# Input casts and transposes moved to the DMA in a kernel of attention and a long convolution

## The chip, the cores and the metric

The kernel runs on one core of one Trainium2 chip. The time is that of the device for one execution, in microseconds. Inputs and output lie in the chip's memory (DRAM); the weights and q, k, v are float32, the matrix products take bfloat16 operands.

## What is computed

```python
# attention: B=4, H=8, S=768, D=64; heads 0, 2 and 6 causal, the others
# causal with only the first 4 keys and a window of 64 kept
scores = (q @ k.T) / 8
a = softmax(where(mask[head], scores, -1e9))
x = (a @ v)                  # [4, 8, 768, 64] -> [4, 768, 512]
# second part: D=512
proj = x @ w_proj            # [512, 1536]
x1, x2, x3 = split(proj, 3)
conv = irfft(rfft(x2, axis=seq) * rfft(filter, axis=seq))
out = (x1 * conv * x3) @ w_out
```

## The kernel before

**Attention.** Two heads of one batch make a pair; there are 16 pairs, four for each batch, and the main loop runs over them. For each pair `emit_loads` (L99) brings q, k and v as float32 on the queue of SyncE (SP), with a sequence position on each partition: 128 partitions, six tiles of 128 positions. `emit_cast` (L269) turns q and k into bfloat16 with the two heads side by side, on VectorE. `emit_prep` (L284) makes `qkT`, in which the 2 x 64 head dimensions lie on the partitions and the 768 positions along the row: six 128x128 TensorE transposes into a PSUM bank for q and six for k, each followed by a VectorE copy into SBUF. `emit_v` (L275) casts v on POOL into `v_aug`, which has a column of ones, and multiplies by a head mask into `v_far`.

`emit_chunk` (L293) computes scores for four 128x128 blocks of both heads at a time (six chunks in a pair), takes the exponential on ScalarE into `pT`, and multiplies the masked blocks on VectorE. `emit_values` (L323) multiplies with v, in which the column of ones gives the sum, and divides on VectorE into `attn`. `emit_turn` (L341) transposes `attn` with six TensorE transposes and a VectorE copy into a quarter of `xT`, the transposed attention output of a batch.

**Second part.** `moe` (L349) is a generator that is advanced one step after each chunk, so that its work for batch b-1 lies among the attention of batch b. It folds the sequence in two (`xf`, two VectorE additions), projects x2 (L358), transforms it with the real matrix `G` (`emit_forward`, L212), multiplies by the transformed filter `HAB`, computes x1 and x3 and their product (L390, L399), transforms back with `Gi` (L406), multiplies, projects (L419) and stores on SP (L423). A batch has 22 steps, about the length of four and a half pairs. After the last pair the second part of the last batch runs alone.

**Setup.** `G` holds sines and cosines that ScalarE computes from iotas made by POOL. `Gi` is made from `G` by 18 TensorE transposes and three VectorE copies (L226). The transformed filter `HAB` comes from `setup_steps` (L225), a generator that starts with the third pair.

**Order.** Within each engine and each queue instructions start in the order that a scheduler derives from the order of the program and the dependences; VectorE and POOL have the written order in the setup. An instruction that waits holds up all that is queued behind it on its engine or queue. The buffers of loaded inputs are three, of `qkT`, `v_aug` and `attn` two. The loads of pair n+2 are issued in pair n (L462). The weights and the filter, which a DMA casts to bfloat16, are issued on POOL's queue in the second pair; `hold` (L95) writes one element of the destination first, so that such a DMA waits until a given pair's `v_aug` is there. The fifth pair's q load is held in the same way.

```python
if c == (1 if n else 3) and nxt:      # L468: casts of the next pair
if c == 2 and last:                   # L473: emit_turn of the pair before
if c == (3 if n else 4) and nxt:      # L477: qkT of the next pair
```

Of the kernel before, what the change touches and what calls it, by code (L numbers as in the profile page):

```python
# [9 lines left out]
FP32 = mybir.dt.float32  # L10
BF16 = mybir.dt.bfloat16
# [32 lines left out]
def kernel(  # L44
# [13 lines left out]
    nc = tc.nc  # L58
# [33 lines left out]
    ret_i64 = const.tile([128, H], mybir.dt.int64, name="ret_i64")  # L92
    nc.sync.dma_start(out=ret_i64, in_=is_retrieval.partition_broadcast(128))

    def hold(first, n):  # L95

        nc.gpsimd.tensor_copy(out=first, in_=state[n]["v_aug"][:, 0, 0, 0:1])

    def emit_loads(b, hp, behind=None):  # L99
        qk = ald.tile([128, 2, 2, NT, D], FP32, name="qk_f32")  # L100
        vf = ald.tile([128, 2, NT, D], FP32, name="v_f32")
        if behind is not None:
            hold(qk[:, 0, 0, 0, 0:1], behind)
        for dst, src in ((qk[:, 0], q), (qk[:, 1], k), (vf, v)):
            nc.sync.dma_start(
                out=dst, in_=src[b, 2 * hp:2 * hp + 2].rearrange("h (t p) d -> p h t d", p=128))
        return qk, vf

    PREFETCH = 2
# [93 lines left out]
    def emit_matrix():  # L203

        nc.gpsimd.tensor_scalar(out=G[:, :, 1, 0], in0=par.to_broadcast([128, NM]), scalar1=-2.0, scalar2=1.0,
                                op0=ALU.mult, op1=ALU.add)
        nc.gpsimd.tensor_copy(out=G[:, :, 6:8, 0:64], in_=G[:, :, 4:6, 64:128])
        nc.gpsimd.tensor_copy(out=G[:, :, 6:8, 64:128], in_=G[:, :, 4:6, 0:64])

    Gi = const.tile([128, 6, HS], BF16, name="Gi")  # L210

    def emit_forward(src, tiles):  # L212

# [9 lines left out]
    HA, HB = HAB[:, :, 0:2, :], HAB[:, :, 2:4, :]  # L223

    def setup_steps():  # L225
        for t in range(0, 6, 2):  # L226
            ps = bank("gi_ps", [128, 2, HS], BF16)
            for u in range(2):
                for m in range(NM):
                    nc.tensor.transpose(ps[:, u, m * 128:(m + 1) * 128], G[:, m, t + u, :], identity)  # L230
            nc.vector.tensor_copy(out=Gi[:, t:t + 2, :], in_=ps)
            yield
        yield
        yield
        fold = msb.tile([128, 2, NM, DM], BF16, name="fold", tag="x2")
        with tc.issue_after(state[3]["first"].ins):
            nc.vector.tensor_add(fold[:, 0], filt[:, 0:NM, :], filt[:, NM:NT, :])
            nc.vector.tensor_sub(fold[:, 1], filt[:, 0:NM, :], filt[:, NM:NT, :])

        def put(engine, out, in_, w):  # L240
            if engine is nc.scalar:
                engine.activation(out=out, in_=in_, func=AF.Copy, scale=w / S)
            else:
                engine.tensor_scalar(out=out, in0=in_, scalar1=w / S, scalar2=None, op0=ALU.mult)

        for t in range(2):
            ps = emit_forward(fold, ((2 * t, t), (2 * t + 1, t)))
            put(nc.scalar, HAB[:, t, 0:4:3, :], ps, 2.0)
            nc.gpsimd.tensor_scalar(out=HB[:, t, 0, :], in0=HB[:, t, 1, :], scalar1=-1.0, scalar2=None,
                                    op0=ALU.mult)  # L250
            nc.gpsimd.tensor_copy(out=HA[:, t, 1, :], in_=HA[:, t, 0, :])
            if t == 0:
                nc.gpsimd.tensor_scalar(out=HA[0:1, 0, 1, :], in0=HB[0:1, 0, 1, :], scalar1=0.5, scalar2=None,
                                        op0=ALU.mult)
                nc.gpsimd.tensor_scalar(out=HA[0:1, 0, 0, :], in0=HA[0:1, 0, 0, :], scalar1=0.5, scalar2=None,
                                        op0=ALU.mult)
                nc.gpsimd.memset(HB[0:1, 0, :, :], 0.0)
            yield
        plain = emit_forward(fold, ((4, 0), (5, 1)))
        put(nc.scalar, HA[0:64, 2, :, :], plain[0:64, :, :], 2.0)  # L260
        put(nc.vector, HB[64:128, 2, :, :], plain[64:128, :, :], 2.0)
        yield
        swapped = emit_forward(fold, ((6, 0), (7, 1)))
        put(nc.scalar, HA[64:128, 2, :, :], swapped[64:128, :, :], 2.0)
        put(nc.vector, HB[0:64, 2, :, :], swapped[0:64, :, :], -2.0)
        yield


    def emit_cast(engine, st, a):  # L269
        if a == 0:  # L270
            st["bf"] = asb.tile([128, 2, NT, 2, D], BF16, name="qk_bf")
        qk = loads[st["pair"]][0]
        engine.tensor_copy(out=st["bf"][:, a], in_=qk[:, a].rearrange("p hh t d -> p t hh d"))  # L273

    def emit_v(st):  # L275
        vf = loads.pop(st["pair"])[1]
        st["v_aug"] = v_aug = asb.tile([128, NT, 2, 65], BF16, name="v_aug")
        nc.gpsimd.memset(v_aug[:, :, :, 64:65], 1.0)  # L278
        nc.gpsimd.tensor_copy(out=v_aug[:, :, :, 0:64], in_=vf.rearrange("p hh t d -> p t hh d"))
        st["v_far"] = v_far = asb.tile([128, 4, 2, 65], BF16, name="v_far")  # L280
        hp = st["pair"][1]
        nc.gpsimd.tensor_mul(v_far, v_aug[:, 0:4], vmask[:, hp, :, :, None].to_broadcast([128, 4, 2, 65]))  # L282

    def emit_prep(st):  # L284
        st["qkT"] = qkT = asb.tile([128, 2, S], BF16, name="qkT")
        for a in range(2):
            ps = bank("qkT_ps", [128, S], BF16)
            for t in range(NT):
                nc.tensor.transpose(ps[:, t * 128:(t + 1) * 128],  # L289
                                    st["bf"][:, a, t].rearrange("p hh d -> p (hh d)"), identity)  # L290
            nc.vector.tensor_copy(out=qkT[:, a], in_=ps)  # L291

    def emit_chunk(st, c):  # L293
        qkT = st["qkT"]
# [44 lines left out]
                             rec[:, :, None].to_broadcast([128, NT, 64]))  # L339

    def emit_turn(st):  # L341
        ps = bank("xt_ps", [128, S], BF16)
        for i in range(NT):
            nc.tensor.transpose(ps[:, i * 128:(i + 1) * 128],
                                st["attn"][:, i].rearrange("p hh d -> p (hh d)"), identity)
        nc.vector.tensor_copy(out=st["xT"][:, st["pair"][1], :], in_=ps)


    def moe(b, xT):  # L349
# [51 lines left out]
        for cb in range(NC):  # L401
            ch = slice(cb * 128, (cb + 1) * 128)
            ps = bank_pair("c_ps")
            for r in range(2):
                for n, (tile_no, t, u) in enumerate(((2 * r, r, 0), (2 * r + 1, r, 1), (4 + r, 2, r))):
                    nc.tensor.matmul(ps[:, r, 0:HS], lhsT=P[:, t, u, ch], rhs=Gi[:, tile_no, :],  # L406
                                     start=(n == 0), stop=(n == 2))
            evs = msb2.tile([128, HS], FP32, name="evs")
            nc.scalar.copy(out=evs, in_=ps[:, 0, 0:HS])
            conv = msb2.tile([128, S], BF16, name="conv")  # L410
            nc.vector.tensor_add(conv[:, 0:HS], evs, ps[:, 1, 0:HS])  # L411
            nc.vector.tensor_sub(conv[:, HS:S], evs, ps[:, 1, 0:HS])
            nc.vector.tensor_mul(y[:, cb, :], conv, g[:, cb, :])  # L413
            yield
# [10 lines left out]
            yield  # L425


    emit_cast(nc.vector, state[0], 0)
    emit_mask(0)
    emit_mask(1)  # L430
    emit_cast(nc.vector, state[0], 1)
    emit_prep(state[0])
    emit_v(state[0])
    setup_order.__exit__(None, None, None)
    loads[pairs[1]] = emit_loads(*pairs[1])
# [12 lines left out]
    for n, (b, hp) in enumerate(pairs):  # L448
# [11 lines left out]
        for c in range(len(CHUNKS)):  # L460
            emit_chunk(st, c)
            if c == (0 if n < 2 else 3) and n + 2 < len(pairs):  # L462
                loads[pairs[n + 2]] = emit_loads(*pairs[n + 2], behind=3 if n == 2 else None)
            if c == 0 and last:
                emit_values(last, 0)
            if c == 1 and last:
                emit_values(last, 1)
            if c == (1 if n else 3) and nxt:  # L468
                with tc.issue_after(st["first"].ins):
                    for a in range(2):  # L470
                        emit_cast(nc.vector, nxt, a)
                emit_v(nxt)
            if c == 2 and last:  # L473
                emit_turn(last)
                if hp == 0:
                    gates.append(moe(b - 1, last["xT"]))
            if c == (3 if n else 4) and nxt:  # L477
                emit_prep(nxt)
            if c == 4 and n == 1:
                filt = msb.tile([128, NT, DM], BF16, name="filt", tag="xf")  # L480
                hold(filt[:, 0, 0:1], 2)
                nc.gpsimd.dma_start(out=filt, in_=moe_filter_fft.rearrange("(t p) c -> p t c", p=128))
                w = moe_w_proj.rearrange("(c p) n -> p c n", p=128)
                for part in (1, 0, 2):
                    cols = slice(part * DM, part * DM + DM)
                    hold(wproj[:, 0, part * DM:part * DM + 1], 2)
                    nc.gpsimd.dma_start(out=wproj[:, :, cols], in_=w[:, :, cols])
                hold(wout[:, 0, 0:1], 2)
                nc.gpsimd.dma_start(out=wout, in_=moe_w_out.rearrange("(c p) n -> p c n", p=128))
            if c < 5:  # L490
                gate_step()
# [44 lines left out]
```

## Time and profile before

| what | value |
|---|---|
| runs | 260.65, 262.06, 263.44 us; median 262.06 |
| profiled execution | 261.73 us, span 260.0 us |
| granted TensorE clock | 0.958 |
| L289 transposes of q and k, PE | 192, 16.6 us busy |
| L344 transposes of attn, PE | 96, 8.1 us |
| L273 casts of q and k, VectorE | 32, 20.9 us |
| L291 copies into qkT, VectorE | 32, 16.8 us |
| L346 copies into xT, VectorE | 16, 8.8 us |
| L279 casts of v, POOL | 16, 15.1 us |
| q, k and v loads on SP | 48 of 384 KB, median 5.1 to 6.0 us from issue to landing |
| DMA | 28.36 MB, 80,822 packets, 74,912 of them under 512 bytes |

The span reaches from the first to the last instruction. PE is TensorE's matmul side, PEld its weight loads, DVE is VectorE, ACT ScalarE, POOL GpSimd, SP SyncE; a q after an engine's name means its sequencer or queue. A line such as L289 is a line of the kernel. A share of DMA is the mean share of 16 DMA engines; the sum of the packets' times can exceed 1 where the packets of several queues overlap. The chain of work that ended last is followed back from the last instruction to whatever released each step.

### The profile page before, as it was taken

The page shows a single profiled execution, that of the slowest core. Times are in us where ns is not written, and L with a number is a line of the kernel's source. Part 1 is how long each engine was busy: PE and PEld are TensorE (multiplying, and loading weights), DVE is VectorE, ACT ScalarE, POOL GpSimd, SP SyncE. Part 2 cuts the span into 40 slices and gives each one's busy share as a digit, 9 for nine tenths or more (in the row PEclk, how much of TensorE's full clock was granted, in tenths as well). Part 3 has the DMA queues.
Part 4 walks back from the last instruction along what each step waited for, and adds up shares of the span by engine and source line. Part 5 has one row for each costly group of instructions (what it writes and reads, how often), then busy time and mean ns, then how long its engine had stood idle before and what let it go on. Part 6 is the DMA issues. An engine that isn't in the chain of part 4 may idle for free.

```text
span 260.0 us, 4624 instructions
## 1 busy us (share of the span) xinstructions
PE 217.1 (83%) x1898; PEld 111.9 (43%) x1898; DVE 178.9 (69%) x349; ACT 153.7 (59%) x182; POOL 52.3 (20%) x83
## 2 busy tenths in 40 slices
PE   0286957386999899989998999899999998999980
PEld 0134532144344455544445555344445553446530
DVE  4988785079269958994599669983697596065640
ACT  6577443534488565758686567576885622663431
POOL 4536732913021202020204022011110000000000
PEclk9999797859799999999999999999999999999996
DMA  7999999999608095439636390042000000600005
GB/s 139 218 218 211 178 193 197 203 228 186 118 6 179 0 183 107 78 92 320 144 56 132 52 183 3 0 164 81 0 3 0 5 0 0 245 0 0 0 21 223
DMA packets 80822, 28.36 MB, mean 109 GB/s; under 512 B 74912, under 2 KB 77728, under 8 KB 80800
## 3 DMA queue, kind: packets, MB, share of 16 engines
q1 hardware_dynamic: 77904, 25.18, 46.2%
q0 software_dynamic: 2896, 2.88, 6.7%
q8 instruction: 15, 0.25, 0.4%
q14 instruction: 7, 0.06, 0.1%
HBM read 24.65 MB, written 6.29 MB: 119 GB/s over the span
## 4 chain that ended last, share of the span: by engine, by line
PE 45%; DVE 35%; DMA 9%; ACT 7%; issue 2%; ACTq 0%; DVEq 0%
PE x_ps L390 12%; PE x_ps L358 8%; DMA qk_f<-in_q_dram 7%; PE out_ps L419 5%; PE att L330 5%; PE sc L304 5%; DVE pT L317 4%; DVE qk_bf L273 4%; PE X_ps L217 4%; ACT pT L310 3%; DVE y L413 3%; DVE conv L411 3%; PE qkT_ps L289 3%; DVE attn L338 3%; DVE m L379 2%
## 5 line engine op out<-in xcount | busy, mean ns | idle before, releaser
L310 ACT ACTIVATE pT<-sc 128x1024 bf16<-128x1024 f32 x96 | 86.1, 922 | 24.1 <-PE sc L304 23.7
L390 PE MATMUL x_ps<-xT,wproj 128*128 128x384 bf16 x256 | 46.7, 326 | 0.0
L304 PE MATMUL sc<-qkT 64*128 64x512 bf16 (+3 forms) x256 | 36.3, 332 | 2.7 <-DVE qkT L291 1.4
L317 DVE TENSOR_TENSOR pT<-pT,mask 128x1024 bf16<-128x1024 bf16 x32 | 23.7, 741 | 17.4 <-ACT pT L310 17.1
L330 PE MATMUL att<-v_aug,pT 128*128 128x65 bf16 x352 | 31.6, 198 | 2.2 <-DVE pT L317 1.4
L289 PE MATMUL qkT_ps<-identity,qk_bf 128*128 128x128 bf16 x192 | 16.6, 238 | 19.0 <-DVE qk_bf L273 15.6
L330 PEld LDWEIGHTS <-pT 128*128 128x128 bf16 x672 | 25.0, 99 | 15.5 <-issue 4.8
L390 PEld LDWEIGHTS <-wproj 128*128 128x128 bf16 x256 | 23.3, 98 | 14.3 <-issue 1.3
L278 POOL MEMSET v_aug<- 128x12 bf16 x16 | 3.4, 220 | 122.5 <-PE att L330 122.5
L273 DVE CAST qk_bf<-qk_f 128x768 bf16<-128x768 f32 x32 | 20.9, 665 | 9.1 <-DMA qk_f<-in_q_dram 9.1
L419 PE MATMUL out_ps<-wout,y 128*128 128x512 bf16 x96 | 24.0, 380 | 3.7 <-DVE y L413 2.7
L217 PE MATMUL X_ps<-x,G 128*128 128x512 bf16 x96 | 23.6, 379 | 0.5 <-ACT x L361 0.2
L358 PE MATMUL x_ps<-wproj,xf 128*128 128x512 bf16 x96 | 23.7, 393 | 0.3 <-DVE xf L351 0.3
L304 PEld LDWEIGHTS <-qkT 64*128 64x128 bf16 x256 | 10.9, 96 | 30.2 <-issue 25.9
L330 PE MATMUL att<-v_far,pT 128*128 128x65 bf16 x320 | 23.2, 196 | 0.0
L289 PEld LDWEIGHTS <-qk_bf 128*128 128x128 bf16 x192 | 12.7, 105 | 23.3 <-DVE qk_bf L273 16.6
L397 ACT CAST x1s<-x_ps 128x768 bf16<-128x768 f32 x16 | 12.8, 800 | 15.1 <-PE x_ps L390 13.6
L422 ACT COPY o_sb<-out_ps 128x1024 f32<-128x1024 f32 x12 | 12.1, 1012 | 15.4 <-PE out_ps L419 12.5
L399 DVE TENSOR_TENSOR g<-x1s,x_ps 128x768 bf16<-128x768 bf16 x16 | 15.2, 951 | 8.6 <-PE x_ps L390 6.9
L361 ACT CAST x<-x_ps 128x1024 bf16<-128x1024 f32 x12 | 12.2, 1014 | 13.5 <-PE x_ps L358 13.5
L282 POOL TENSOR_TENSOR v_far<-v_aug,vmask 128x520 bf16<-128x520 bf16 x16 | 18.5, 1153 | 1.2
L338 DVE TENSOR_TENSOR attn<-att,rec 128x384 bf16<-128x384 f32 x32 | 17.7, 552 | 0.4
(80 smaller groups left out, 271.6 us busy)
## 6 DMA issues: line engine op xcount, KB each, us to landing
qk_f<-in_q_dram SPq DMA_DIRECT2D x16, 384.0 KB, 5.1
qk_f<-in_k_dram SPq DMA_DIRECT2D x16, 384.0 KB, 6.0
v_f<-in_v_dram SPq DMA_DIRECT2D x16, 384.0 KB, 5.9
out_dram<-o_sb SPq DMA_DIRECT2D x12, 512.0 KB, 2.9
wproj<-in_moe_w_proj_dram POOLq DMA_DIRECT2D x3, 512.0 KB, 15.7
filt<-in_moe_filter_fft_dram POOLq DMA_DIRECT2D x1, 768.0 KB, 9.9
wout<-in_moe_w_out_dram POOLq DMA_DIRECT2D x1, 512.0 KB, 21.0
ret_i<-in_is_retrieval_dram SPq DMA_DIRECT2D x1, 8.0 KB, 3.1
```

What stands on the lines that cost most here:

```text
L217: nc.tensor.matmul(ps[:, u, :], lhsT=G[:, m, t, :], rhs=src[:, r, m, :], start=(m == 0), stop=(m == NM - 1))
L273: engine.tensor_copy(out=st["bf"][:, a], in_=qk[:, a].rearrange("p hh t d -> p t hh d"))
L282: nc.gpsimd.tensor_mul(v_far, v_aug[:, 0:4], vmask[:, hp, :, :, None].to_broadcast([128, 4, 2, 65]))
L289: nc.tensor.transpose(ps[:, t * 128:(t + 1) * 128], st["bf"][:, a, t].rearrange("p hh d -> p (hh d)"), identity)
L304: nc.tensor.matmul(sc[:, hh, n * 128:(n + cnt) * 128], lhsT=qkT[rows, 1, j * 128:(j + 1) * 128], rhs=qkT[rows, 0, i * 128:(i + cnt) * 128] ...
L310: nc.scalar.activation(out=pT[:, :, 512 * c:512 * c + w], in_=sc[:, :, 0:w], func=AF.Exp, scale=SCALE)
L317: nc.vector.tensor_mul(near[:, :, c - 1:c + 1, 0:256], near[:, :, c - 1:c + 1, 0:256], mask[:, h0:h0 + 2, 1, None, :].to_broadcast([128, 2 ...
L330: nc.tensor.matmul(att[:, i, :], lhsT=st["pT"][:, hh, at:at + 128], rhs=st["v_far" if i >= j + 2 else "v_aug"][:, j, hh, :], start=(j == 0 ...
L338: nc.vector.tensor_mul(st["attn"][:, :, hh, :], att[:, :, 0:64], rec[:, :, None].to_broadcast([128, NT, 64]))
L358: nc.tensor.matmul(ps[:, r, :], lhsT=xf[:, cc, r, m * 128:(m + 1) * 128], rhs=wproj[:, cc, DM:2 * DM], start=(cc == 0), stop=(cc == NC - 1))
L390: nc.tensor.matmul(ps[:, s, 0:HS], lhsT=wproj[:, cc, part * DM + cb * 128:part * DM + (cb + 1) * 128], rhs=xT[:, cc, s * HS:s * HS + HS], ...
L419: nc.tensor.matmul(ps[:, n, :], lhsT=y[:, cb, (i + n) * 128:(i + n + 1) * 128], rhs=wout[:, cb, :], start=(cb == 0), stop=(cb == NC - 1))
```

## The change

q and k are loaded by four DMAs per pair on POOL's queue, one for each of q and k and each head, which cast to bfloat16 on the way. One DMA transpose on SP's queue, through the crossbar, makes the whole `qkT` of a pair (twelve 128x128 blocks). The same kind of DMA makes `Gi` (24 blocks, in another layout) and the `xT` quarter of each pair but the last (six blocks). The v casts and the small operations on `HAB` go from POOL to VectorE. The holds are gone, and the filter is loaded in the first pair and the weights earlier in the second. `qkT` of the next pair is called for where its casts were, and the second part of a batch enters one chunk later.

```diff
-    def emit_loads(b, hp, behind=None):
-        qk = ald.tile([128, 2, 2, NT, D], FP32, name="qk_f32")
+    def emit_loads(b, hp):
+        qk = ald.tile([128, 2, NT, 2, D], BF16, name="qk")
         vf = ald.tile([128, 2, NT, D], FP32, name="v_f32")
-        if behind is not None:
-            hold(qk[:, 0, 0, 0, 0:1], behind)
-        for dst, src in ((qk[:, 0], q), (qk[:, 1], k), (vf, v)):
-            nc.sync.dma_start(
-                out=dst, in_=src[b, 2 * hp:2 * hp + 2].rearrange("h (t p) d -> p h t d", p=128))
+        for a, src in ((0, q), (1, k)):
+            for hh in range(2):
+                nc.gpsimd.dma_start(
+                    out=qk[:, a, :, hh], in_=src[b, 2 * hp + hh].rearrange("(t p) d -> p t d", p=128))
+        nc.sync.dma_start(
+            out=vf, in_=v[b, 2 * hp:2 * hp + 2].rearrange("h (t p) d -> p h t d", p=128))
         return qk, vf
...
+        nc.sync.dma_start_transpose(out=Gi.rearrange("p m t f -> p (m t) f"),
+                                    in_=G.rearrange("p m t f -> p (m t f)"))
-    Gi = const.tile([128, 6, HS], BF16, name="Gi")
+    Gi = const.tile([128, NM, 8, 128], BF16, name="Gi")
...
     def setup_steps():
-        for t in range(0, 6, 2):
-            ps = bank("gi_ps", [128, 2, HS], BF16)
-            for u in range(2):
-                for m in range(NM):
-                    nc.tensor.transpose(ps[:, u, m * 128:(m + 1) * 128], G[:, m, t + u, :], identity)
-            nc.vector.tensor_copy(out=Gi[:, t:t + 2, :], in_=ps)
-            yield
-        yield
-        yield
+        for _ in range(5):
+            yield
...
-            nc.gpsimd.tensor_scalar(out=HB[:, t, 0, :], in0=HB[:, t, 1, :], scalar1=-1.0, scalar2=None,
+            nc.vector.tensor_scalar(out=HB[:, t, 0, :], in0=HB[:, t, 1, :], scalar1=-1.0, scalar2=None,
...
-        nc.gpsimd.tensor_copy(out=v_aug[:, :, :, 0:64], in_=vf.rearrange("p hh t d -> p t hh d"))
+        nc.vector.tensor_copy(out=v_aug[:, :, :, 0:64], in_=vf.rearrange("p hh t d -> p t hh d"))
...
     def emit_prep(st):
         st["qkT"] = qkT = asb.tile([128, 2, S], BF16, name="qkT")
-        for a in range(2):
-            ps = bank("qkT_ps", [128, S], BF16)
-            for t in range(NT):
-                nc.tensor.transpose(ps[:, t * 128:(t + 1) * 128],
-                                    st["bf"][:, a, t].rearrange("p hh d -> p (hh d)"), identity)
-            nc.vector.tensor_copy(out=qkT[:, a], in_=ps)
+        nc.sync.dma_start_transpose(
+            out=qkT.rearrange("p a (t s) -> p (a t) s", t=NT),
+            in_=loads[st["pair"]][0].rearrange("p a t hh d -> p (a t hh d)"))
...
     def emit_turn(st):
-        ps = bank("xt_ps", [128, S], BF16)
-        for i in range(NT):
-            nc.tensor.transpose(ps[:, i * 128:(i + 1) * 128],
-                                st["attn"][:, i].rearrange("p hh d -> p (hh d)"), identity)
-        nc.vector.tensor_copy(out=st["xT"][:, st["pair"][1], :], in_=ps)
+        if st is state[len(pairs) - 1]:
+            ps = bank("xt_ps", [128, S], BF16)
+            for i in range(NT):
+                nc.tensor.transpose(ps[:, i * 128:(i + 1) * 128],
+                                    st["attn"][:, i].rearrange("p hh d -> p (hh d)"), identity)
+            nc.vector.tensor_copy(out=st["xT"][:, st["pair"][1], :], in_=ps)
+            return
+        nc.sync.dma_start_transpose(
+            out=st["xT"][:, st["pair"][1], :].rearrange("p (t s) -> p t s", t=NT),
+            in_=st["attn"].rearrange("p t hh d -> p (t hh d)"))
...
-                    nc.tensor.matmul(ps[:, r, 0:HS], lhsT=P[:, t, u, ch], rhs=Gi[:, tile_no, :],
+                    nc.tensor.matmul(ps[:, r, 0:HS], lhsT=P[:, t, u, ch], rhs=Gi[:, :, tile_no, :],
...
-                loads[pairs[n + 2]] = emit_loads(*pairs[n + 2], behind=3 if n == 2 else None)
+                loads[pairs[n + 2]] = emit_loads(*pairs[n + 2])
...
             if c == (1 if n else 3) and nxt:
-                with tc.issue_after(st["first"].ins):
-                    for a in range(2):
-                        emit_cast(nc.vector, nxt, a)
+                emit_prep(nxt)
                 emit_v(nxt)
             if c == 2 and last:
                 emit_turn(last)
-                if hp == 0:
-                    gates.append(moe(b - 1, last["xT"]))
-            if c == (3 if n else 4) and nxt:
-                emit_prep(nxt)
-            if c == 4 and n == 1:
+            if c == 3 and last and hp == 0:
+                gates.append(moe(b - 1, last["xT"]))
+            if c == 1 and n == 0:
                 filt = msb.tile([128, NT, DM], BF16, name="filt", tag="xf")
-                hold(filt[:, 0, 0:1], 2)
                 nc.gpsimd.dma_start(out=filt, in_=moe_filter_fft.rearrange("(t p) c -> p t c", p=128))
+            if c == 1 and n == 1:
                 w = moe_w_proj.rearrange("(c p) n -> p c n", p=128)
                 for part in (1, 0, 2):
                     cols = slice(part * DM, part * DM + DM)
-                    hold(wproj[:, 0, part * DM:part * DM + 1], 2)
                     nc.gpsimd.dma_start(out=wproj[:, :, cols], in_=w[:, :, cols])
-                hold(wout[:, 0, 0:1], 2)
                 nc.gpsimd.dma_start(out=wout, in_=moe_w_out.rearrange("(c p) n -> p c n", p=128))
```

More of the change, by code (lines that the diff above doesn't have):

```diff
@@ L93 @@
     nc.sync.dma_start(out=ret_i64, in_=is_retrieval.partition_broadcast(128))
-    def hold(first, n):
-        nc.gpsimd.tensor_copy(out=first, in_=state[n]["v_aug"][:, 0, 0, 0:1])
-    def emit_loads(b, hp, behind=None):
-        qk = ald.tile([128, 2, 2, NT, D], FP32, name="qk_f32")
+    def emit_loads(b, hp):
+        qk = ald.tile([128, 2, NT, 2, D], BF16, name="qk")
         vf = ald.tile([128, 2, NT, D], FP32, name="v_f32")
-        if behind is not None:
-            hold(qk[:, 0, 0, 0, 0:1], behind)
-        for dst, src in ((qk[:, 0], q), (qk[:, 1], k), (vf, v)):
-            nc.sync.dma_start(
-                out=dst, in_=src[b, 2 * hp:2 * hp + 2].rearrange("h (t p) d -> p h t d", p=128))
+        for a, src in ((0, q), (1, k)):
[4 more added lines that the diff above has]
+            out=vf, in_=v[b, 2 * hp:2 * hp + 2].rearrange("h (t p) d -> p h t d", p=128))
         return qk, vf
@@ L248, in setup_steps @@
             put(nc.scalar, HAB[:, t, 0:4:3, :], ps, 2.0)
-            nc.gpsimd.tensor_scalar(out=HB[:, t, 0, :], in0=HB[:, t, 1, :], scalar1=-1.0, scalar2=None,
+            nc.vector.tensor_scalar(out=HB[:, t, 0, :], in0=HB[:, t, 1, :], scalar1=-1.0, scalar2=None,
                                     op0=ALU.mult)
-            nc.gpsimd.tensor_copy(out=HA[:, t, 1, :], in_=HA[:, t, 0, :])
+            nc.vector.tensor_copy(out=HA[:, t, 1, :], in_=HA[:, t, 0, :])
             if t == 0:
-                nc.gpsimd.tensor_scalar(out=HA[0:1, 0, 1, :], in0=HB[0:1, 0, 1, :], scalar1=0.5, scalar2=None,
+                nc.vector.tensor_scalar(out=HA[0:1, 0, 1, :], in0=HB[0:1, 0, 1, :], scalar1=0.5, scalar2=None,
                                         op0=ALU.mult)
-                nc.gpsimd.tensor_scalar(out=HA[0:1, 0, 0, :], in0=HA[0:1, 0, 0, :], scalar1=0.5, scalar2=None,
+                nc.vector.tensor_scalar(out=HA[0:1, 0, 0, :], in0=HA[0:1, 0, 0, :], scalar1=0.5, scalar2=None,
                                         op0=ALU.mult)
-                nc.gpsimd.memset(HB[0:1, 0, :, :], 0.0)
+                nc.vector.memset(HB[0:1, 0, :, :], 0.0)
             yield
@@ L266, in setup_steps @@
         yield
[L269 to L273, printed above, removed]
     def emit_v(st):
@@ L425, in moe @@
             yield
-    emit_cast(nc.vector, state[0], 0)
+    emit_prep(state[0])
     emit_mask(0)
     emit_mask(1)
-    emit_cast(nc.vector, state[0], 1)
-    emit_prep(state[0])
     emit_v(state[0])
```

## The prediction

> **What bounds the kernel now.** I read the busy times of the page first, then the same busy times by stage, then the chain of work that ended last, then the DMA queues inside the stage where the chain waits for a transfer.
>
> Busy times:
>
> ```profile
> PE 217.1 (83%) x1898; PEld 111.9 (43%) x1898; DVE 178.9 (69%) x349; ACT 153.7 (59%) x182; POOL 52.3 (20%) x83
> ```
>
> TensorE leads, VectorE follows. That average hides two different kernels, which the stages show (start and end in us, length, busy us of each engine, granted clock, DMA share, GB/s):
>
> ```profile
> 13.00:38.00 25.00, 19.22 (x242) 12.02 (x243) 20.77 (x43) 16.46 (x19) 13.09 (x21) 0.93 1.22 200
> 38.00:52.00 14.00, 7.05 (x34) 2.39 (x33) 4.89 (x7) 5.80 (x6) 9.10 (x9) 0.83 1.11 200
> 52.00:65.00 13.00, 9.31 (x95) 5.63 (x95) 10.61 (x20) 5.22 (x6) 3.16 (x4) 0.76 1.14 207
> 65.00:115.00 50.00, 47.30 (x435) 24.12 (x434) 38.50 (x77) 32.52 (x40) 8.37 (x12) 0.97 0.49 95
> 115.00:165.00 50.00, 48.18 (x468) 25.08 (x466) 38.58 (x77) 35.53 (x43) 8.39 (x12) 1.00 0.55 119
> 165.00:216.00 51.00, 48.98 (x438) 24.47 (x437) 38.00 (x76) 32.25 (x39) 4.03 (x6) 1.00 0.08 32
> 216.00:260.00 44.00, 35.43 (x180) 17.07 (x180) 17.93 (x30) 17.88 (x21) 0.00 (x0) 0.95 0.19 72
> ```
>
> Up to 65 us the DMA share is above 1 (queues overlap) at a flat 200 GB/s, with TensorE half idle between 38 and 52. From 65 to 216 TensorE is busy 144.5 of 151 us and DMA has half or more to spare. From 216 the last batch's second part runs alone.
>
> The chain confirms the first stage:
>
> ```profile
> 32.37 1.29 DVE pT L317
> 33.65 0.07 DVE xT L346
> 33.72 17.70 DMA qk_f<-in_q_dram
> ...
> 51.52 0.79 DVE qk_bf L273
> 52.36 1.46 PE qkT_ps L289 x12
> ```
>
> One q load, that of the fifth head pair, is the path for 17.70 us; the median q load lands in 5.1. The queues between 13 and 52 us say why:
>
> ```profile
> q1 hardware_dynamic: 19173, 4.86, 72.8%
> q0 software_dynamic: 2896, 2.88, 44.9%
> ```
>
> The weights, on POOL's queue, take 44.9% of 39 us of the 16 engines beside the inputs.
>
> **What the Trainium skill says.** "DMA: Bandwidth & Descriptors", section "Issuing engines are not separate DMA queues": transfers of all issuers end on the same 16 engines and interleave. The 17.70 us beside the weights agree. The same page, section "Latency and other measured facts", gives crossbar transposes an effective 261 GB/s; "VectorE: DVE Perf Modes", section "The three transpose paths", gives 1309 ns for one 128x128 bf16 block by the crossbar. They price one block at 32 KB / 261 = 0.126 us or at 1.309 us, a factor of ten; this trace holds no crossbar transpose and can't choose. The DMA page's "SWDGE vs HWDGE vs iDMA" says that a casting DMA must come from GpSimd, whose cores compute the descriptors; the filter's load here holds POOL 1.05 us for 128x6 = 768 rows, which agrees.
>
> **The change, part by part.**
>
> *TensorE and VectorE.* Gone from TensorE: L289 16.6 us, 15 of 16 of L344's 8.1, L230 1.8: 26.0 busy us. Only those from 65 to 216 us lie on a TensorE-bound path. By stage, qkT_ps has 2.53 + 3.88 + 2.30 = 8.71 there and xt_ps 1.75 + 2.31 + 2.03 = 6.09, of which 0.51 (the last pair's) stays: 14.3 us. VectorE loses the casts of q and k (20.9), the copies of qkT (16.8), of xT (15/16 of 8.8) and of Gi (1.6), 47.5 in all. It gains the v casts, 16 x 0.665 (the q/k cast row, same shape) = 10.6, and seven small operations for HAB, at most POOL's 8.4 us for them, at least some 3 (an estimate from L197's 0.444 us for 128x512). Net 28 to 34 us less. VectorE is 35% of the chain but not its floor, so I count its relief only as what lets TensorE's gain through: 0.7 of 14.3 = 10 us gained, between 5 (the chain stays with VectorE and ScalarE, whose largest row, exp, has 86.1 us and isn't touched) and 14.3.
>
> *POOL.* Four q/k DMAs a pair, each of 128x6 rows as the filter's, 1.05 us: 4.2 a pair, 67 in all. It loses the v casts (15.1), HAB (8.4) and the holds (1.9): about 94 us of 260, hidden in sum. In order, it matters: the first pair's four DMAs stand ahead of the iotas. Those move from 0.9 to about 5 us, and the masks and angles with them. The exp waited until 13.65 us for scores, while its tables were ready at 9.38 + 1.28 = 10.7; shifted by 4.2 that is 14.9, +1.2. On the data side, the last issue ends at 5.0, the shortest landing of such a load is 3.4, and the transpose adds 12 x 0.126 = 1.5 and about 2.0 of fixed time (an estimate; the DMA page's fit, its stores here land in 2.9): 12, against 12.95 now. I take **+1**; bounds 0 and, at 1.309 a block, +13.
>
> *DMA in the first stage.* The q/k load keeps its 256-byte reads and row count, so I leave its engine time at today's: q1 has 77,904 packets in 46.2% of 16 x 260 us, 24.7 ns each, so a pair's 4,608 rows cost 7.1 us of all 16 engines. (Half-size writes might save something, descriptors made by software might cost; bounds 20% each way, 5 pairs x 4.7 x 0.2 = 5 us.) Five pairs and the weights (6.7% of 260 = 17.4) give 53 us, which is when the fifth pair's q lands: the first stage is DMA time, and what is added to it is paid. Added ahead of the fifth pair's qkT: five q/k transposes of 12 blocks, Gi of 24, two or so xT of 6, 96 blocks. At 0.126 that is **+12**. Further, weights and q/k now share POOL's queue, so the fifth pair's loads (issued later) go behind all weights in place of beside them. The weights end at 28.6 + 21.0 = 49.6 now and that q at 51.4, so the order costs little: **+1**. The removed cast, transposes and copy after landing (about 3.5 us from 51.5) are balanced by the transpose's own 3.5.
>
> *DMA from 65 us on.* Twelve pairs of 18 blocks x 0.126 = 27 us in a stretch where the shares leave 151 - (0.49 x 50 + 0.55 x 50 + 0.08 x 51) = 95 us free: hidden. That cover ends at 95/216 = 0.44 us a block.
>
> *SP's queue and xT.* SP, in order, now carries v loads, q/k transposes, xT transposes and the stores. An xT transpose waits for attn, and stands behind the next pair's q/k transpose, which waits for that pair's four loads. The old way, six transposes (0.51) and a copy (0.55), took 1.1 us plus waits; the new one 6 x 0.126 + 2.0 = 2.8, plus up to 3.5 for the transpose ahead and 0.5 to 1.7 for a v load's issue: 2 to 7 us later. Three of four xT aren't needed at once. The fourth feeds xf, and the moe steps now begin one chunk later, which covers about 12.6/6 = 2.1 us. The xf additions wait on VectorE with the pT masks queued behind them, for which the att matmuls wait. So 0 to 5 us a batch for three batches; I take 2: **+6**. The fourth batch keeps its TensorE transpose.
>
> *Gi and the tail.* Gi is read in three runs of 128 columns; c_ps has no wait of its own, so nothing, 0 to 1 us. From 216 us nothing changes. Issuing the filter and weights earlier, without holds, moves DMA within a full stage: nothing, bounds -3 (TensorE has setup work to fill its idle 7 us with) to +4 (they delay the third and fourth pair).
>
> Sum, on the profiled execution's own 261.7 us (span 260.0 and 1.7 around it; the median of the runs is 262.06, so the same number within 0.1%): 261.7 + 1 + 13 - 10 + 6 = **272 us**.
>
> **Rivals.**
> 1. *The first stage swallows the transposes: faster.* The shares above 1 show queues overlapping on the engines; if a load's 24.7 ns a row is mostly waiting on memory, SBUF-to-SBUF tiles slip between, and weights that start earlier pay the rest. Then the first stage adds 0, xT's wait is covered by attention work, and all 14.3 us come: 261.7 + 1 - 14.3 = 248; with 2 us of waits, 250. It decides when a block costs the loads under about 0.04 us: (10 - 6 - 1)/96 is 0.03, and 0.1 if xf costs nothing. Against it: 200 GB/s stayed flat whatever was queued. Chance 0.22.
> 2. *The crossbar is the bound.* With the geometric middle of the two prices, 0.41 us: first stage 96 x 0.41 = 39, start +2, order +1, xf 3 x 4 = 12, and the steady gain is eaten since 0.41 is next to the 0.44 limit: 316. At the full 1.309 its 306 blocks alone last 400 us, and the kernel some 440. Speaking for it: the second price is for one block of exactly this kind; against it, one block alone includes fixed time that 96 in a row share. Chance 0.26.
> 3. *The parts cancel.* Gain 13 against 13, within 1%: 0.08, besides a little from the forecast's lower edge.
>
> **How the numbers follow.** The forecast's case, 265 to 290, has 0.44. A run differs from no change by about 1% (259.4 to 264.7) before it can be told. Faster 0.22 from rival 1; same 0.08 and 0.02 from the edge; slower 0.42 + 0.26 = 0.68. The range leaves out the fastest third of rival 1 (0.07) and the slow part of rival 2 (0.11): 249 to 320. The forecast's own range is 265 to 290.
>
> **What would show it.** Right: the chain's DMA piece before the fifth pair lasts past 60 us, and the first moe matmul (L358, now 65.4) starts at 76 to 80; a 12-block transpose lands in 3.5 to 6 us; from there to the end takes about 185 us in place of 195; TensorE's busy time is near 191, VectorE's near 148; VectorE shows waits for an xT DMA, three of a few us. Rival 1 shows L358 by 67; rival 2 shows transposes that land in 8 us or more, and scores that wait for qkT in every pair. What would make me wrong: a load rate of casting DMAs well off 24.7 ns a row, or one transpose stuck on SP behind a store that waits for ScalarE, which would stop all qkT behind it.

## The result and the profile after

The changed kernel takes 269.33 us (median; 268.73 to 270.87), the kernel before on the same chip 261.36. The ratio is 1.034, with a 95% interval of 1.025 to 1.043: slower. The profiled execution has 269.9 us and a span of 268.2.

The engines' busy times, after:

```profile
PE 199.7 (74%) x1598; PEld 98.2 (37%) x1598; DVE 153.3 (57%) x290; ACT 152.8 (57%) x182; POOL 80.6 (30%) x118
```

TensorE has 17.4 us less work than before, VectorE 25.6 us less, and the kernel is longer. The same stages as before the change (start and end, length, busy us of PE, PEld, DVE, ACT and POOL, clock, DMA share, GB/s) show where the time went:

```profile
13.00:38.00 25.00, 9.44 (x80) 4.99 (x80) 13.66 (x31) 16.73 (x21) 14.71 (x22) 0.95 1.60 179
38.00:52.00 14.00, 3.56 (x43) 2.35 (x43) 1.01 (x3) 1.94 (x2) 0.76 (x1) 0.50 1.28 189
52.00:65.00 13.00, 7.39 (x70) 4.16 (x68) 7.07 (x15) 5.00 (x6) 8.76 (x12) 0.71 1.91 158
65.00:115.00 50.00, 40.95 (x339) 18.93 (x338) 32.25 (x56) 32.82 (x39) 18.61 (x23) 0.86 1.32 123
115.00:165.00 50.00, 46.68 (x412) 23.12 (x409) 37.16 (x67) 37.12 (x45) 19.52 (x26) 1.00 1.27 154
```

Between 13 and 52 us TensorE did 26.3 us of work before; now it does 13.0. The chain of work that ended last (start, length, what) names what it waits for:

```profile
13.97 1.24 DMA filt<-in_moe_filter_fft_dram
15.21 12.42 DMA qkT<-qk
27.67 1.51 PE sc L287 x7
...
32.61 15.78 DMA qkT<-qk
49.38 0.91 PE sc L287 x5
50.29 8.91 DMA qkT<-qk
...
76.54 4.74 DMA xT<-attn
81.37 0.97 DVE xf L339
82.39 3.61 PE x_ps L346 x8
```

Three q/k transposes, those of the second, third and fourth pair, of 12.4, 15.8 and 8.9 us take the place of the single load of 17.70 us. TensorE's score matmuls waited 34.3 us for `qkT`:

```profile
L287 PE MATMUL sc<-qkT 64*128 64x512 bf16 (+3 forms) x256 | 37.4, 342 | 42.9 <-DMA qkT<-qk 34.3
```

The first matmul of the second part (L346, before L358) starts at 82.4 us in place of 65.4. From it to the end takes 185.8 us in place of 194.6. So the first stage lost 17.0 us and all the rest won 8.8: together the 8.2 by which the span grew.

The first start of that matmul divides all runs below, and "first stage" means the time up to it. It is read from its first weight load, since a trace can lack a few matmul records. "The rest" is the span less that. Each of these stage times is read from one profiled execution; the four runs of a kernel lie 1.3 to 4.7 us apart, so a difference of a microsecond or two between two kernels' stages says little by itself.

### The profile page after: what moved, and what is told of

Its sections match the earlier page's. It is cut to its first block, busy times and chain, and to the rows that moved or that the text cites. A ratio compares the mean times of both kernels' runs of the same rounds, so it can differ in the third digit from the quotient of the medians.

```text
span 268.2 us, 4095 instructions
## 1 busy us (share of the span) xinstructions
PE 199.7 (74%) x1598; PEld 98.2 (37%) x1598; DVE 153.3 (57%) x290; ACT 152.8 (57%) x182; POOL 80.6 (30%) x118
## 4 chain that ended last, share of the span: by engine, by line
PE 42%; DVE 21%; DMA 17%; ACT 11%; POOL 4%; issue 3%; ACTq 0%; POOLq 0%; DVEq 0%
DMA qkT<-qk 14%; PE x_ps L378 12%; PE x_ps L346 8%; PE att L313 6%; PE out_ps L407 6%; PE sc L287 5%; ACT pT L293 4%; PE X_ps L216 4%; DVE pT L300 4%; POOL qk L100 3%; DVE conv L399 3%; DVE y L401 2%; DVE conv L400 2%; DVE m L365 2%; DMA xT<-attn 2%
## 5 line engine op out<-in xcount | busy, mean ns | idle before, releaser
L287 PE MATMUL sc<-qkT 64*128 64x512 bf16 (+3 forms) x256 | 37.4, 342 | 42.9 <-DMA qkT<-qk 34.3
L100 POOL DMA_DIRECT2D qk<-in_q_dram x32 | 26.9, 843 | 68.2 <-DMA qkT<-qk 65.0
L300 DVE TENSOR_TENSOR pT<-pT,mask 128x1024 bf16<-128x1024 bf16 x32 | 25.8, 806 | 28.2 <-ACT pT L293 28.2
L313 PE MATMUL att<-v_aug,pT 128*128 128x65 bf16 x352 | 36.3, 206 | 7.3 <-DVE pT L300 4.2
L313 PEld LDWEIGHTS <-pT 128*128 128x128 bf16 x672 | 28.8, 105 | 24.8 <-DVE pT L300 8.4
L346 PE MATMUL x_ps<-wproj,xf 128*128 128x512 bf16 x96 | 24.3, 402 | 4.3 <-DVE xf L339 4.2
L100 POOL DMA_DIRECT2D qk<-in_k_dram x32 | 27.0, 850 | 0.2
L313 PE MATMUL att<-v_far,pT 128*128 128x65 bf16 x320 | 25.9, 206 | 0.0
L268 POOL TENSOR_TENSOR v_far<-v_aug,vmask 128x520 bf16<-128x520 bf16 x16 | 18.8, 1175 | 11.7 <-DVE v_aug L265 11.6
L410 ACT COPY o_sb<-out_ps 128x1024 f32<-128x1024 f32 x12 | 12.2, 1013 | 14.7 <-PE out_ps L407 11.5
L385 ACT CAST x1s<-x_ps 128x768 bf16<-128x768 f32 x16 | 12.8, 800 | 13.5 <-PE x_ps L378 13.5
L365 DVE TENSOR_TENSOR m<-X,HAB 128x1024 bf16<-128x1024 bf16 x12 | 9.8, 815 | 16.1 <-ACT X L355 16.1
L394 PE MATMUL c_ps<-Gi,P 128*128 128x384 bf16 x96 | 17.6, 326 | 1.5 <-DVE g L387 1.2
L298 DVE TENSOR_TENSOR pT<-pT,mask 128x512 bf16<-128x512 bf16 x16 | 6.7, 416 | 20.0 <-ACT pT L293 20.0
```

The lines of the kernel that those rows point to most:

```text
L100: nc.gpsimd.dma_start(out=qk[:, a, :, hh], in_=src[b, 2 * hp + hh].rearrange("(t p) d -> p t d", p=128))
L287: nc.tensor.matmul(sc[:, hh, n * 128:(n + cnt) * 128], lhsT=qkT[rows, 1, j * 128:(j + 1) * 128], rhs=qkT[rows, 0, i * 128:(i + cnt) * 128] ...
L300: nc.vector.tensor_mul(near[:, :, c - 1:c + 1, 0:256], near[:, :, c - 1:c + 1, 0:256], mask[:, h0:h0 + 2, 1, None, :].to_broadcast([128, 2 ...
L313: nc.tensor.matmul(att[:, i, :], lhsT=st["pT"][:, hh, at:at + 128], rhs=st["v_far" if i >= j + 2 else "v_aug"][:, j, hh, :], start=(j == 0 ...
L346: nc.tensor.matmul(ps[:, r, :], lhsT=xf[:, cc, r, m * 128:(m + 1) * 128], rhs=wproj[:, cc, DM:2 * DM], start=(cc == 0), stop=(cc == NC - 1))
```

## The experiments

Three theories stood at the start. Theory 1, the forecast's: the transposes' DMA time in the first stage is the cost. Theory 2: the casting loads, through POOL's queue or their rows, are the cost. Theory 3: ScalarE's order at the start is, with an exp ahead of the sines of G.

**The two halves apart.** The change has two parts that can stand alone: loads that cast, and transposes by the crossbar. One kernel keeps only the first (the v casts and HAB stay on VectorE):

```diff
-        nc.sync.dma_start_transpose(
-            out=qkT.rearrange("p a (t s) -> p (a t) s", t=NT), ...)
+        for a in range(2):
+            ps = bank("qkT_ps", [128, S], BF16)
+            for t in range(NT):
+                nc.tensor.transpose(ps[:, t * 128:(t + 1) * 128], st["bf"][:, a, t].rearrange("p hh d -> p (hh d)"), identity)
+            nc.vector.tensor_copy(out=qkT[:, a], in_=ps)
...
-        if st is state[len(pairs) - 1]:
+        if True:
```

with Gi from TensorE and qkT called for as late as before.

> Only the casting loads stay; qkT, xT and Gi are transposed on TensorE again. Theory 1 (the transposes' DMA time in the first stage costs the kernel its time): the first moe matmul, at 82.4 us in the changed kernel, comes back to 65 to 70, TensorE's 14 us are not gained from there on, total 260 to 264. Theory 2 (the casting loads on POOL's queue, and their rows, are the cost): it stays at 75 to 82 us and the total rises to 270 to 278. Theory 3 (the order of ScalarE at the start, exp ahead of the sines, is the cost): the order depends on when the scheduler has qkT, so either the sines are first again and the total is 260 to 264, or exp is first and it's 268 to 275.

It took 251.96 us, 0.968 (0.962 to 0.975) of the kernel before: faster than any of the three theories had it. Its two parts:

```profile
0.00:58.40 58.40, 31.97 (x385) 19.27 (x389) 45.57 (x97) 36.03 (x42) 41.72 (x66) 0.99 1.50 165
58.40:250.00 191.60, 177.04 (x1498) 90.90 (x1511) 125.78 (x244) 117.31 (x140) 38.86 (x52) 0.99 0.42 65
```

The first stage is 58.4 us, 7.0 less than before. Theory 2 falls: it had the stage at 75 to 82. Theory 1 had it at 65 to 70 and no place for a gain.

The other kernel keeps only the crossbar:

```diff
-        qk = ald.tile([128, 2, NT, 2, D], BF16, name="qk")
+        qk = ald.tile([128, 2, 2, NT, D], FP32, name="qk_f32")
...
-                nc.gpsimd.dma_start(out=qk[:, a, :, hh], ...)
+            nc.sync.dma_start(out=dst, in_=src[b, 2 * hp:2 * hp + 2]...)
...
+                with tc.issue_after(st["first"].ins):
+                    for a in range(2):
+                        emit_cast(nc.vector, nxt, a)
```

> Only the crossbar transposes stay; q and k are loaded as float32 on SP and cast on VectorE. Theory 1: first moe matmul still at 78 to 84 us, total 268 to 274 (VectorE has 20.9 us of casts back, little of it on the path). Theory 2: first moe matmul at 65 to 70, total 252 to 258. Theory 3: as theory 1 if exp is still ahead of the sines, else 258 to 264.

268.14 us, 1.030 (1.021 to 1.039), with a first stage of 84.9 us, a microsecond past theory 1's 78 to 84. This kernel isn't a clean half: with no q/k loads and no holds on POOL, its queue was free at once, and the filter was issued at 1.88 us, ahead of most inputs. So the same kernel was run with the holds (that of the fifth pair's q too) and the weights' place of the kernel before:

```diff
+                hold(filt[:, 0, 0:1], 2)
                 nc.gpsimd.dma_start(out=filt, ...)
...
+                    hold(wproj[:, 0, part * DM:part * DM + 1], 2)
                     nc.gpsimd.dma_start(out=wproj[:, :, cols], in_=w[:, :, cols])
```

> The kernel with the crossbar alone (float32 loads on SP, casts on VectorE), with the weights, the filter and the fifth pair's q held back as in the kernel before, since without holds the weights came ahead of the first pairs' inputs. Theory 1: the transposes' cost without the loads' gain, first moe matmul at 85 to 90 us, total 268 to 276. Rival (the crossbar alone is cheap and the early weights were what cost the first crossbar kernel its time): first moe matmul at 70 to 76, total 256 to 263.

269.40 us, 1.032 (1.026 to 1.037), and a first stage of 81.2 us. As in the changed kernel the chain waits for transposes, and at one point also for SP's own queue, where the issue of a v load took 9.91 us:

```profile
37.94 9.91 SPq L105
47.96 9.46 DMA qkT<-qk_bf
...
77.00 3.21 DMA xT<-attn
80.23 0.97 DVE xf L348
82.08 2.78 PE x_ps L355 x6
```

The total is as theory 1 said; the first stage is 4 us better than its lower end. The casts were given a counterpart, since their kernel also issued the weights earlier and without holds: the kernel with casts alone, with the filter and the weights issued and held as in the kernel before. The hold of the fifth pair's q wasn't put back.

> The kernel with casts alone, with the filter and the weights issued and held back where the kernel before has them. Theory (the casting loads themselves bring the 7 us of the first stage): first moe matmul at 56 to 61 us, total 250 to 254. Rival (the earlier filter and weights bring them): first moe matmul at 64 to 68, total 256 to 260.

251.61 us, 0.968 (0.961 to 0.975), first stage 58.4 again. So the place of the filter and the weights doesn't bring the gain. The casting loads do, or something that came with them; the last part of this section returns to it. The two halves and their sum, first stage / the rest / median:

| | transposes on TensorE | transposes by the crossbar |
|---|---|---|
| float32 loads, cast on VectorE | 65.4 / 194.6 / 261.4 | 81.2 / 184.6 / 269.4 |
| casting loads | 58.4 / 191.9 / 252.0 | 82.4 / 185.8 / 269.3 |

(The upper left cell is the kernel before. It had medians of 259.9 to 261.4 beside the other runs. The upper cells have the holds, the lower ones don't. In all but the upper left v's casts and the small operations on `HAB` are on VectorE and the second part enters one chunk later.) The crossbar costs the first stage 15.8 us alone and 24.0 beside the casting loads. The half with the casts saves 7.0 us alone and nothing beside the crossbar.

**How the cost follows the number of blocks.** Two kernels take some of the transposes back to TensorE. One makes Gi there:

```diff
-        nc.sync.dma_start_transpose(out=Gi.rearrange("p m t f -> p (m t) f"), ...)
...
+                    nc.tensor.transpose(ps[:, u, m * 128:(m + 1) * 128], G[:, m, t + u, :], identity)
+            nc.vector.tensor_copy(out=Gi[:, t:t + 2, :], in_=ps)
```

> The changed kernel with Gi made by TensorE as before: 24 of the 96 blocks that the crossbar moves in the first stage are gone. Theory 1: first moe matmul 3 to 6 us earlier, total 264 to 267. Theories 2 and 3: no change, 268 to 271.

267.51 us, and a first stage of 78.6 us: 3.8 less than the changed kernel, within what theory 1 said of the stage and half a microsecond above its total. The total alone (1.029, 1.020 to 1.037) can't be told from the changed kernel's. The other makes Gi and xT on TensorE and leaves qkT:

```diff
-        if st is state[len(pairs) - 1]:
+        if True:
```

> The changed kernel with xT and Gi on TensorE, so that only qkT goes over the crossbar: 72 of 120 blocks before the first moe matmul. Theory 1 (0.2 us a block): first moe matmul at 58.8 + 14 = 73, total 259 to 264. Rival (each transpose is dear by its turn on SP's queue, behind others that wait, and not by its blocks): 64 to 69, total 253 to 258.

264.10 us, first stage 72.6, as theory 1 had it; the total lies at the upper edge of its range. The blocks that the crossbar moved before the mark are counted from SP's queue: none, 72, 96 and 120 (six qkT, Gi, four xT) for casts alone, qkT only, without Gi, and the changed kernel. The first stages are 58.4, 72.6, 78.6 and 82.4: 14.2/72, 20.2/96 and 24.0/120 are 0.20, 0.21 and 0.20 us a block. Beside float32 loads the same 120 blocks cost 15.8 us, 0.13 each. So the cost grows with the blocks, and no single transpose makes it. What a block pays for is less sure. Counted by transposes (6, 10 and 11) the same three costs are 2.4, 2.0 and 2.2 us each, a somewhat worse fit and no more. Nor need it all be time of the 16 engines. SP's queue is held too: the third transpose on the chain was issued only when an xT transpose ahead of it had gone.

```profile
38.48 11.59 SPq L332 DMA_TRANSPOSE xT<-attn  x1
50.29 3.74 SPq L272 DMA_TRANSPOSE qkT<-qk  x1
```

And the fifth pair's last k load was issued at 52.52 us, behind a small write to `v_aug` on POOL that had waited 13.5 us for the attention matmuls. No run separates the engines' time from these turns in the queues.

What a transpose costs alone can be read in the changed kernel's late stage. Between 188 and 196 us one is issued at 191.19, and nothing else runs beside it (DMA share in tenths and GB/s in 40 slices of 0.2 us):

```profile
DMA  9999000000000000000000999999999300000000
GB/s 451 369 451 369 0 0 0 0 0 0 0 0 0 0 0 0 0 0 0 0 0 14 191 220 211 210 206 216 227 186 220 66 0 0 0 0 0 0 0 0
...
qkT<-qk SPq DMA_TRANSPOSE x1, 3.7
```

It starts to move data about 1 us after its issue and moves for some 2.0 us, most slices at 190 to 220 GB/s, 0.17 us a block, with nobody to contend with; the store in the first slices goes at 370 to 450.

**The start on ScalarE.** In the changed kernel the first exp was placed ahead of ScalarE's work on G, so masks and the first masked product came late (before, this product started at 14.71 us):

```profile
22.76 0.42 DVE L298 TENSOR_TENSOR pT<-pT,mask 128x512 bf16<-128x512 bf16 x1
```

The edit puts the exps behind the sines:

```diff
+        with tc.issue_after(last_sine.ins):
             nc.scalar.activation(out=pT[:, :, 512 * c:512 * c + w], in_=sc[:, :, 0:w],
```

> The changed kernel with the exps put behind the sines of G on ScalarE; nothing else is edited. The first masked product moves from 22.8 to about 15 to 17 us. Theory 1: the first stage is DMA time, so an earlier start only lengthens a later wait: first moe matmul at 79 to 83, total 266 to 270. Theory 3: it comes back by 6 to 8 us, to about 75, total 261 to 264.

The product moved to 18.53 us, not to the 15 to 17 expected: 4.2 of the 8 us came back. The first stage stayed at 82.2 and the total at 270.52 (1.039, 1.031 to 1.047), half a microsecond above theory 1's range. A start 4 us earlier was only waited for later; theory 3, which had the stage come back by 6 to 8 us, falls. Whether the other 4 us would count wasn't tried.

**The crossbar only where DMA has room.** If the first stage is where the crossbar costs, and TensorE's relief comes later, the two can be had apart: casting loads for all pairs, TensorE for qkT of the first six pairs, xT of the first five and Gi, the crossbar for the rest.

```diff
+    def emit_prep(st):
+        (prep_pe if st["n"] < 6 else prep_xbar)(st)
...
-        if st is state[len(pairs) - 1]:
+        if st["n"] < 5 or st is state[len(pairs) - 1]:
```

> Casting loads for every pair, as in the changed kernel; qkT of the first six pairs, xT of the first five and Gi on TensorE, all later qkT and xT on the crossbar. Theory 1 (the crossbar's blocks cost some 0.2 us of saturated DMA each in the first stage and are hidden later): the first moe matmul stays near the 58.8 us of the kernel with casts alone, and the rest is 4 to 7 us shorter than its 191.9, total 244 to 249. Rival (a crossbar transpose costs as much in the steady stage, through SP's queue and waits for xT): total 251 to 256.

244.55 us, 0.938 (0.933 to 0.943) of the kernel before. First stage 58.6, the rest 184.4: 7.5 us less than with casts alone. Its two parts:

```profile
0.00:59.00 59.00, 34.43 (x386) 20.89 (x390) 47.86 (x98) 36.29 (x42) 42.81 (x67) 0.96 1.49 163
59.00:243.00 184.00, 166.75 (x1318) 81.66 (x1329) 114.31 (x213) 117.09 (x140) 37.94 (x52) 0.98 0.69 99
```

TensorE is busy 166.8 us there, against 177.0 for casts alone, 10.3 less; the rest is 7.5 us shorter. VectorE has lost its copies too, 11.5 us (114.3 against 125.8), and no run tells which engine's relief counts.

xT of each batch's fourth pair is the one that xf waits for. It was put back on TensorE too:

```diff
-        if st["n"] < 5 or st is state[len(pairs) - 1]:
+        if st["n"] < 5 or st["pair"][1] == HP - 1:
```

> The hybrid, with the xT of each batch's fourth pair on TensorE too, since xf needs it at once. Theory (a crossbar xT makes xf, and the masked products behind it on VectorE, wait 2 us a batch): 1 to 4 us less than the hybrid, 241 to 244. Rival (attention work covers that wait): the same as the hybrid or 1 us more, 244 to 246.

243.95 us, 0.930 (0.923 to 0.938): no difference from the hybrid that these runs can tell. So that wait costs nothing that shows here.

The cover later was tried by doing each late qkT a second time:

```diff
+        spare = asb.tile([128, 2, S], BF16, name="spare")
+        nc.sync.dma_start_transpose(out=spare.rearrange("p a (t s) -> p (a t) s", t=NT), ...)
```

> The hybrid, with each of its ten late qkT transposes done a second time into a tile that nothing reads: 120 blocks more, none in the first stage. Theory 1 (after the first stage DMA has room): total 244 to 248. Rival (the crossbar costs SP's queue or DMA as much later as in the first stage, 0.2 us a block): 260 to 268.

260.43 us, 16 more than the hybrid, so the theory's number failed. But the experiment didn't do what it was meant to. SP's queue between 50 and 74 us, and the longest of its waits:

```profile
50.29 1.37 SPq L290 DMA_TRANSPOSE spare<-qk  x1
51.76 1.24 SPq L102 DMA_DIRECT2D v_f<-in_v_dram  x1
59.76 1.44 SPq L290 DMA_TRANSPOSE spare<-qk  x1
61.30 0.80 SPq L102 DMA_DIRECT2D v_f<-in_v_dram  x1
69.26 1.43 SPq L290 DMA_TRANSPOSE spare<-qk  x1
70.74 2.87 SPq L286 DMA_TRANSPOSE qkT<-qk  x1
...
SPq L290 <- DMA qk<-in_k_dram: 75.9, 16, 13.9
```

The useless transposes have no reader and no buffer to wait for, and the scheduler put them two pairs ahead: three stand before the first useful qkT. Each waits at the head of SP's queue for a load (75.9 us in all), with a qkT behind it. This shows what transposes out of order on SP can cost; whether DMA would have had the time for 120 more blocks stays open.

**What brings the 7 us of the half with the casts.** Two guesses were tried. If it's the bytes written, v should gain as well:

```diff
-        nc.sync.dma_start(out=vf, in_=v[b, 2 * hp:2 * hp + 2]...)
+        for hh in range(2):
+            nc.gpsimd.dma_start(out=vf[:, :, hh], in_=v[b, 2 * hp + hh]...)
```

> The kernel with casts alone, with v loaded by two casting DMAs a pair too (into a bfloat16 tile, and copied by VectorE). Theory (the first stage follows the bytes that DMA writes, which the cast halves): first moe matmul 2 to 4 us earlier than 58.8, total 248 to 250. Rival (it follows the 256-byte rows, or POOL's issue, 1.7 us more a pair): first moe matmul at 59 to 63, total 252 to 257.

255.48 us, 3.5 more than with casts of q and k alone, as the rival had it; the first stage, 63.8, lies 0.8 above even the rival's range. In that stage

```profile
0.00:63.80 63.80, 33.18 (x386) 20.22 (x389) 48.17 (x97) 36.23 (x42) 57.06 (x85) 1.00 1.48 122
```

POOL, which issues these loads at some 0.85 us each, is busy 57.1 of 63.8 us (41.7 of 58.4 with q and k alone), so this can be POOL's limit and doesn't clear the bytes. The other guess: two queues carry the inputs in place of one. The kernel before, with only v moved to POOL's queue as float32:

```diff
-        for dst, src in ((qk[:, 0], q), (qk[:, 1], k), (vf, v)):
-            nc.sync.dma_start(
+        for dst, src, eng in ((qk[:, 0], q, nc.sync), (qk[:, 1], k, nc.sync), (vf, v, nc.gpsimd)):
+            eng.dma_start(
```

> The kernel before, with one edit: v (float32, no cast) is issued on POOL's queue in place of SP's, so that the inputs' rows are spread over two queues. Theory 2 (the first stage is a count of packets, some 645 a us where the inputs share one queue and some 715 where two carry them, whatever their bytes): first moe matmul at 58 to 61 us in place of 65.4, total 253 to 257. Rival (the casting loads save because they write half the bytes): first moe matmul at 64 to 68, total 259 to 264.

264.98 us, 1.016 (1.011 to 1.021), first stage 67.9: the second queue brings nothing here, though v's loads then also take their turn among POOL's other work. Its packets fell to 57,781 from 80,822 for the same 28.36 MB, at no gain, so a count of packets isn't the measure either.

The reason for the 7 us stays open, with three candidates. Half the bytes are written for q and k. The q/k casts left VectorE, some 5 us of the chain of the kernel before up to 65.4 us. And the hold of the fifth pair's q is gone. In the kernel before VectorE waits for this load:

```profile
DVE qk_bf L273 <- DMA qk_f<-in_q_dram: 9.1, 1, 9.1
```

It was issued at 33.72 us there. In the kernel with casts and held weights that pair's four loads are issued between 21.3 and 24.6 us, ahead of the weights, and from 13 us to the end of the first stage neither TensorE nor VectorE waits for a load. The kernel before without this hold, which could tell the hold from the casts, wasn't run.

## Why the prediction was right, and where it wasn't

The forecast was 272 with its own range of 265 to 290; measured, 269.33. The direction and the place are the forecast's: the transposes lengthen the first stage, TensorE's relief comes after it and is smaller. That the sum came so near is in part luck, since misses cancelled, within the first stage and between it and the rest. Step by step:

- *The first stage, +14.* Measured +17.0, with the mark at 82.4 us and not at 76 to 80. One term that was mis-sized is the number of blocks: 96 were taken as ahead of the fifth pair's qkT, but the first matmul of the second part has 120 before it, since SP's order puts the sixth pair's qkT and all four xT there. At the forecast's 0.126 us these are 15.1; the crossbar alone cost 15.8, or 0.13 us each. Here the 261 GB/s that the Trainium skill gives in "DMA: Bandwidth & Descriptors", section "Latency and other measured facts" (for a non-contiguous middle dimension), did well. It did less well alone (0.17 us a block) and beside casting loads (0.20), and these are what the changed kernel has: its blocks cost 24.0 us, twice the forecast's 12, less the 7.0 of the half with the casts, which the forecast put at 0. The 1.309 us of "VectorE: DVE Perf Modes", section "The three transpose paths", is no price per block: six blocks in one DMA land here in 2.7 us and twelve in 3.7 when the engines are free. The forecast's 2.0 of fixed time was near: 3.7 less the 2.0 of moving is 1.7.
- *Load rows at today's price, 0.* If the loads bring the 7 us, this is wrong by more than the bound given (5 us). Beside the crossbar the same half saves nothing, so the total didn't show it: luck.
- *Start, +1.* The masks came 8 us later, not 4, for a reason that wasn't foreseen (the exp ahead of G's activations). Taking back 4.2 of the 8 us changed nothing.
- *TensorE, -10 and xT, +6.* The rest became 8.8 us shorter, as against 4 in the sum and the 10 of the section on what to look for. The transposes' own busy time there fell as forecast, from 8.71 + 6.09 to 0.50 us, 14.3 less. But TensorE's busy time fell only by 179.8 - 169.0 = 10.8 us, since the spans of matmuls overlap: the times by output tile add up to 198.6 us before and 184.8 after, so 18.8 us of overlap became 15.9. This is 3.5 of the 8.7 us by which TensorE's 199.7 lies above the 191 of the section on what to look for; the others lie in the first stage and weren't followed up. VectorE has 153.3, not 148. The wait for xT, +6, was overestimated, and this is why the rest came out 4.8 us better than the sum had it, against the 3.0 by which the first stage came out worse: xf waited 4.1 us in two cases, 3.7 of it once, at the end of the first stage and so already in the 17.0; in the hybrid, taking the fourth xT off the crossbar was worth nothing measurable.
- *The later cover.* It held with the change's own blocks: the hybrid has 180 of the 306 blocks in that stage and gained there. DMA's share rose to 1.32 and 1.27 from 0.49 and 0.55, so the cover was thinner than the 95 us of free time suggested (the first of these stretches still holds 17 us of the first stage).
- *Waits in place.* A transpose was forecast to land in 3.5 to 6 us. The median is 5.0, but those that decided, in the first stage, took 9 to 16. The two longest, 12.4 and 15.8, ran while the filter or the weights were in flight; the third, 8.9, came after them.

Rival 1 needed a block under 0.04 us and had 0.13 to 0.20; rival 2 needed some 0.4. Rival 2's sign, landings of 8 us and more, did show for qkT, but only in the first stage; after it they took 3.7 to 5.1 us.

## What to carry to other kernels

Here work moved from a busy engine to DMA paid only in the stages where DMA had time; in the stage full of loads each transposed block cost 0.13 to 0.20 us. Read the profile by stage and make the change stage by stage: with transposes on TensorE until the loads have caught up, and on the crossbar after, the same change goes from 3% slower to 6% faster. When a change has two halves, run each alone: here one half was worth 3% and the other hid it.

## What the runs showed that wasn't expected

With loads that cast float32 to bfloat16, and the transposes left on TensorE, the first stage took 58.4 us in place of 65.4, though they read the same 256-byte rows; whether the casts or what came with them did it is open. A crossbar transpose with nothing beside it moved 393 KB in some 2.0 us, about 200 GB/s, where a plain store shortly before it reached 370 to 450. And beside weight loads the same 12 blocks took up to 15.8 us to land, against 3.7 with the DMA engines free.
